# Moving the SBUF tiles of an attention and feed-forward kernel to multiples of 128 bytes

## The chip, the core and the metric

The kernel runs on one core of one Trainium2 chip. The metric is the device time of one execution in microseconds (us): the median of several runs. TensorE (PE) multiplies matrices and writes to PSUM; VectorE (DVE) and ScalarE (ACT) do the element-wise work; SyncE (SP) issues nearly all DMAs; GpSimd (POOL) does a little at the start. SBUF is the on-chip memory that all of them read: 128 partitions, and an address in bytes along each. Every tile has one address, the same in all partitions.

## The reference

Two attention steps, one after the other, and a feed-forward layer on the result, all in float32:

```python
p_packed = sm_attn(p, k, v)                 # 32 packed queries per head attend to k, v
out = sm_attn(q, p_packed, p_packed)        # 576 queries per head attend to the packed rows
x = out.transpose(0, 2, 1, 3).reshape(8 * 576, 512)
h = x @ w_in                                # 512 -> 2048
g = h * (1 / (1 + exp(-1.702 * h)))
return g @ w_out                            # 2048 -> 512
```

There are 8 batches (`b`), 8 heads of 64 columns, and 4608 tokens in all.

## The kernel before

The order of all work is written out by hand in one long table, `order`, of steps such as `(prod, 1, 4, 1, 2, "D")`; a loop at its end calls them one by one, and each engine executes its own instructions in that order. Tiles come from a pool, `wk`, by a tag with a number of buffers: the buffers of a tag lie at fixed SBUF addresses and are used in turn. In the kernel before, a tag gets its addresses at its first use, right behind the tags used earlier, rounded up to 32 bytes.

The feed-forward layer is done in two phases, `ph` 0 and 1, of half of the 2048 hidden columns each, and each phase in four parts `u` of 256 hidden columns. For every phase, batch and half of a batch's 576 tokens (`half`), and every `u`:

- `h_mm` (line 699) makes h in PSUM: 2 times 6 matmuls. The moving operand, which streams through TensorE, is 288 columns of a tile `a` (the attention weights of the second step, split in an upper and a lower part); the stationary operand, which is loaded into TensorE ahead of the matmul, is 128 columns of a tile `m` (packed values times `w_in`, split likewise).
- ScalarE writes the gated result to a tile `X` (line 719); VectorE forms four sums in `X` (line 769); ScalarE and VectorE split the seven blocks of `X` into an upper and a lower part in a tile `gs` (lines 111 and 789).
- `prod` (line 860) multiplies seven blocks of `gs` with seven combinations of the blocks of `w_out`, four in a tile `Wa` and three in a tile `Wb`, by three matmuls each, since both are split: 21 matmuls, into four PSUM banks A to D. The stationary operand is 128 columns of `gs`, the moving one 256 columns of `Wa` or `Wb`. There is one `Wa` and one `Wb` tile for each `u` (tags `Wa0` to `Wa3`, `Wb0` to `Wb3`), and `prod(..., u, "B")` is always six matmuls on the `Wb` tile of that `u`. Tokens 257 to 288 of each half are gathered from several batches as `over` and go the same way.

Batches 1 to 7 give 14 sets of tokens in each phase (two halves each) and the `over` tokens two more (one for every four batches): 16, so 128 passes through `prod` (2 phases, 16 sets, 4 parts), so 2688 matmuls of line 860: 1536 on `Wa`, 1152 on `Wb`. Batch 0 takes a simpler way, `prod0` (line 816): 192 matmuls of 512 moving columns from `Wa`. `h_mm` makes 1536 matmuls.

Around them stand the smaller steps: `m_mm` (line 547, moving operand `w_in`), the scores, softmaxes and transposes of attention (tiles `x`), and DMAs. `k`, `q`, `v` and the partial results of phase 0 are loaded into the two buffers of tag `kqv`; weights come in as `raw`; partial results leave from `r`; four batches send their transposed attention weights through DRAM in pieces of 128 bytes a partition (`aside`).

These are the places, in bytes past a multiple of 256, of the tiles that matter, in the built program of before:

| tile | before |
|---|---|
| `gs` (3 buffers), `X` (3), `r` (2), `PT` (8), `aT` | 128 |
| `Wa0` to `Wa3`, `Wb0`, `Wb1` | 192 |
| `Wb2` | 64 |
| `Wb3` | 128 |
| `m` (3), `a` (3), `x` (6), `kqv` (2), `over` (4) | 192 |
| `raw` (2) | 64 |
| `w_in` (2), `ident`, `minus` | 128 |

All blocks inside these tiles that a matmul of line 860 reads begin at multiples of 512 bytes from the tile's start; the second half of an `a` tile begins 1152 bytes into it, that is 128 past a multiple of 256. The `gs` tile of the very last pass through `prod` is an exception: it takes a buffer of tag `m`.

Of the kernel before, what the change touches and what calls it, by code (L numbers as in the profile page):

```python
# [8 lines left out]
F32 = mybir.dt.float32  # L9
# [12 lines left out]
def kernel(  # L22
# [33 lines left out]
    P = 128  # L56
    D = P // 2
    DM, DF = w_in.shape
    NP = DM // P
    B = q.shape[0]  # L60
    S = q.shape[2] // NP
    NPK = pk.shape[2] // NP - S
    NH = S // 2
    G = S // NPK
    FC = 512
    HC = FC // 2
    CF = FC // P
    KC = (S + P - 1) // P
# [4 lines left out]
    ABUFS, XBUFS, GBUFS, RBUFS = 3, 3, 3, 2  # L73
# [3 lines left out]
    wk = ctx.enter_context(tc.tile_pool(name="wk", bufs=1))  # L77
    ps_acc = ctx.enter_context(tc.tile_pool(name="ps_acc", bufs=1, space=PSUM))
    ps_h = ctx.enter_context(tc.tile_pool(name="ps_h", bufs=2, space=PSUM))
    dram = ctx.enter_context(tc.tile_pool(name="dram", bufs=1, space=bass.MemoryType.DRAM))  # L80

    ident = cst.tile([P, P], F32, name="ident")
    make_identity(nc, ident)
# [84 lines left out]
    raw = {}  # L168
# [1604 lines left out]
```

## Time and profile before

| | us |
|---|---|
| median of 3 runs | 672.59 |
| lowest and highest run | 672.45, 673.4 |
| span of the profiled execution | 672.0 |
| TensorE matmul busy in that span | 658.8 (98%) |
| VectorE busy | 555.0 (83%) |
| ScalarE busy | 409.3 (61%) |

The span is the time from the first to the last instruction of one profiled execution; the runs lie 0.4 to 1.4 us above it. In the rows below, start times count from the start of the span. The busy time of a matmul contains its way through the array, in which the next one already runs. So the pace of TensorE is not read from the length of a matmul (the profile gives about 0.28 us for one of 256 columns) but from start to start.

### The profile page before, as it was taken

To read this page: it belongs to the slowest core of one execution; us is meant where nothing else is said; L and a number is where in the kernel's file an instruction comes from. 1 tells how busy PE (TensorE), PEld (TensorE's weight loads), DVE (VectorE), ACT (ScalarE), POOL (GpSimd) and SP (SyncE) were. 2 spreads that over 40 slices of the span, in tenths; PEclk is the share of its full clock that TensorE was granted. 3 is DMA by queue.
4 is the path that set the end of the run, shared out by engine and by line. 5 is a ranking of instruction groups with operands and counts; after the bars stand their busy time and mean duration, and the time that the engine had idled before them with its cause. 6 is when DMAs were issued, how large, how long until landed. Compare 5 with 4: busy or idle time off the path is not lost.

```text
span 672.0 us, 15271 instructions
## 1 busy us (share of the span) xinstructions
PE 658.8 (98%) x6227; PEld 598.2 (89%) x6227; DVE 555.0 (83%) x1132; ACT 409.3 (61%) x738; POOL 5.4 (1%) x15
## 2 busy tenths in 40 slices
PE   8999899999999999999999999999999999999996
PEld 6777698988989899898999799999999999999996
DVE  3969988879799796987999846878898878886897
ACT  5878777858677695886978554444443544434441
POOL 2100000000000000000000000000000000000000
PEclk9999999999999999999999999999999999999999
DMA  9885646745465476463785315141252222233221
GB/s 342 306 283 182 228 95 222 200 166 217 110 243 144 163 232 188 156 182 137 259 292 187 128 36 155 54 173 50 82 180 88 87 88 87 62 112 87 87 88 63
DMA packets 59174, 104.92 MB, mean 156 GB/s; under 512 B 31392, under 2 KB 36128, under 8 KB 58208
## 3 DMA queue, kind: packets, MB, share of 16 engines
q1 hardware_dynamic: 58960, 103.81, 47.3%
q8 instruction: 49, 0.80, 0.5%
q14 instruction: 21, 0.17, 0.1%
q10 hardware_dynamic: 144, 0.13, 0.1%
HBM read 70.51 MB, written 33.42 MB: 155 GB/s over the span
## 4 chain that ended last, share of the span: by engine, by line
PE 79%; DMA 7%; DVE 7%; ACT 4%; SPq 2%; issue 1%; DVEq 0%; ACTq 0%
PE h L699 25%; PE accC L860 11%; PE accA L860 11%; PE accB L860 10%; PE accD L860 6%; PE psm_None L547 4%; DMA raw_in_None<-w_in 2%; PE accA_over L860 2%; PE accB_over L860 2%; DMA home_m<-w_in 1%; PE accC_over L860 1%; PE ps L591 1%; DMA aT<-aside 1%; PE pspv_None L496 1%; DMA home<-w_in 1%; PE accD L816 1%
## 5 line engine op out<-in xcount | busy, mean ns | idle before, releaser
L699 PE MATMUL h<-a,m 128*128 128x288 f32 x1536 | 223.8, 296 | 2.5 <-ACT x L111 1.3
L699 PEld LDWEIGHTS h<-a,m 128*128 128x128 f32 x1536 | 208.2, 188 | 8.2 <-ACT x L111 2.9
L111 ACT CAST gs<-X 128x896 fp32r<-128x896 f32 (+2 forms) x117 | 104.6, 902 | 75.8 <-DVE X L769 17.8
L789 DVE TENSOR_TENSOR gs<-X,gs 128x896 fp32r<-128x896 f32 x112 | 120.8, 1086 | 22.8 <-ACT gs L111 22.3
L719 ACT ACTIVATE X<-h 128x512 f32<-128x512 f32 (+1 forms) x129 | 76.1, 597 | 83.4 <-PE h L699 77.7
L769 DVE TENSOR_TENSOR X<-X 128x256 f32<-128x256 f32 (+1 forms) x336 | 104.6, 330 | 21.6 <-ACT X L719 17.2
L860 PE MATMUL accC<-Wa,gs 128*128 128x256 f32 x672 | 98.1, 281 | 0.0
L860 PE MATMUL accB<-Wb,gs 128*128 128x256 f32 x672 | 97.7, 281 | 0.0
L860 PEld LDWEIGHTS accC<-Wa,gs 128*128 128x128 f32 x672 | 87.3, 188 | 5.2 <-issue 4.3
L860 PEld LDWEIGHTS accB<-Wb,gs 128*128 128x128 f32 x672 | 87.3, 188 | 1.9 <-issue 0.9
L860 PE MATMUL accA<-Wa,gs 128*128 128x256 f32 x336 | 59.0, 284 | 0.0
L860 PE MATMUL accD<-Wa,gs 128*128 128x256 f32 x336 | 58.5, 282 | 0.0
L860 PE MATMUL accA<-Wb,gs 128*128 128x256 f32 x336 | 57.8, 280 | 0.0
L860 PEld LDWEIGHTS accA<-Wa,gs 128*128 128x128 f32 x336 | 47.7, 188 | 5.4 <-issue 5.1
L860 PEld LDWEIGHTS accD<-Wa,gs 128*128 128x128 f32 x336 | 48.0, 188 | 4.6 <-issue 2.2
L111 ACT CAST m<-psm_None 128x1024 fp32r<-128x1024 f32 x31 | 30.8, 1016 | 29.4 <-PE psm_None L547 29.0
L860 PEld LDWEIGHTS accA<-Wb,gs 128*128 128x128 f32 x336 | 47.5, 188 | 0.0
L571 DVE TENSOR_TENSOR m<-psm_None,m 128x1024 fp32r<-128x1024 f32 x31 | 37.3, 1217 | 6.7 <-ACT m L111 6.5
L725 ACT ACTIVATE over<-h 128x64 f32<-128x64 f32 x128 | 35.3, 289 | 0.0
L547 PE MATMUL psm_None<-w_in,PT 64*32 64x512 f32 x496 | 32.6, 596 | 0.8 <-DVE x L601 0.8
L665 DVE TENSOR_TENSOR a<-xt,a 128x576 fp32r<-128x576 f32 x31 | 23.1, 745 | 2.5 <-ACT a L111 2.1
L719 ACT ACT_TABLE_LOAD x17 | 21.8, 1283 | 4.3 <-PE h L699 3.0
(203 smaller groups left out, 794.4 us busy)
## 6 DMA issues: line engine op xcount, KB each, us to landing
part<-r SPq DMA_DIRECT2D x14, 896.0 KB, 5.4
p<-part SPq DMA_DIRECT2D x14, 896.0 KB, 5.5
q<-q SPq DMA_DIRECT2D x16, 576.0 KB, 5.4
o<-r SPq DMA_DIRECT2D x16, 512.0 KB, 3.5
raw_out_None<-w_out SPq DMA_DIRECT2D x16, 511.8 KB, 5.6
v<-v SPq DMA_DIRECT2D x7, 1024.0 KB, 5.6
raw_in_None<-w_in SPq DMA_DIRECT2D x12, 511.8 KB, 4.8
k<-pk SPq DMA_DIRECT2D x8, 640.0 KB, 4.0
```

Of the source, the lines that this page charges most:

```text
L111: nc.scalar.copy(dst, src)
L496: nc.tensor.matmul(bank[32 * j : 32 * j + 32, e, e * D : (e + 1) * D], turned()[:, c, e, 32 * j : 32 * j + 32], vt[:, c, e0 : e0 + D], sta ...
L547: nc.tensor.matmul(banks[eo][32 * j : 32 * j + 32], PT[rows(eo), j, :], w_in_sb[c % 2][rows(eo), j, at], start=True, stop=True,)
L571: nc.vector.tensor_tensor(m[:, 1, :, at], st["bank", "m", b, c, part], m[:, 0, :, at].bitcast(F32), op=ALU.subtract,)
L591: nc.tensor.matmul(bank[32 * j : 32 * j + 32, eo, :NH], st["PT", b][rows(eo), j, :], kq["q0", half][rows(eo), j, :] if b == 0 else kq["q", ...
L665: engine.tensor_tensor(even_odd(a[:, 1], eo), even_odd(st["t", 2, b, half], eo), even_odd(a[:, 0], eo).bitcast(F32), op=ALU.subtract,)
L699: nc.tensor.matmul(h, m[:, part, eo, at], a[:, ap, eo * NH : (eo + 1) * NH], start=(n == 0), stop=(n == len(terms) - 1), skip_group_check= ...
L719: nc.scalar.activation(X[:, :4].rearrange("p (f t) n -> p f (t n)", f=2)[:, chunks(f)], st["h", *k][:, chunks(f), :NM], AF.Gelu_apprx_sigm ...
L725: nc.scalar.activation(over_part(ph, b, half, u), st["h", ph, b, half, u][:, :, NM:NH], AF.Gelu_apprx_sigmoid, scale=2.0,)
L769: engine.tensor_tensor(to, a, b_, op=ALU.subtract)
L789: engine.tensor_tensor(lo, X, hi.bitcast(F32), op=ALU.subtract)
L860: nc.tensor.matmul(acc[:, n * HC : (n + 1) * HC], gs[:, gp, g], Wa[:, wp, w] if w < 4 else Wb[:, wp, w - 4], start=(u == 0 and n == 0 and ...
```

## The change

Right after the pools are opened, a table `places` takes all buffers of all tags of the pool once, in a chosen order, before the first instruction: the tags of a few bytes first, then a pad of 16 words (64 bytes), then the large ones. That fixes the addresses; nothing is written to or read from these first tiles. Every later use of a tag gets its buffers in the same turn as before.

```diff
     dram = ctx.enter_context(tc.tile_pool(name="dram", bufs=1, space=bass.MemoryType.DRAM))
+
+    places = (
+        ("mx1", 2, 2), ("nb1", 2, 2), ("sm1", 2, 2), ("again", 1, 2), ("rs1", 1, 4), ("rsa", 1, 2),
+        ("mx2", G, 2), ("sm2", G, 2), ("rs2", G, 2), ("pad0", 16, 1),
+        ("kqv", KC * DM, 2), ("x", S, 6), ("Wb2", 6 * HC, 1),
+        ("gs", 14 * P, GBUFS), ("aT", KC * 2 * P, 1), ("X", 8 * P, XBUFS),
+        ("r", 7 * HC, 2), ("pn", 2 * D, 1), ("PT", P, 8), ("Wb3", 6 * HC, 1), ("raw", 2 * FC, RBUFS),
+        ("Wb0", 6 * HC, 1), ("m", 4 * FC, 3),
+    )
+    for tag, words, bufs in places:
+        for i in range(bufs if words else 0):
+            wk.tile([P, words], F32, tag=tag, name=f"place_{tag}_{i}", bufs=bufs)
```

The tags that are not in the table (`Wa0`, `a`, `Wb1`, `over0`, `Wa1` and so on) follow behind `m` in the order of their first use, as before. In the built program every instruction, its engine, its place in the order, its shape and its waits are the same; addresses alone differ. Every tile of the table above now lies at a multiple of 256 bytes, apart from `w_in`, `ident` and `minus`, which stay at 128 past one. The small tiles (maxima, sums and their reciprocals) move by a multiple of 128 bytes. No tile changes its size or its number of buffers.

## Rows read from the trace of the kernel before

**Rows 1.** Page, the chain that ended last, share of the span by engine.

```profile
PE 79%; DMA 7%; DVE 7%; ACT 4%; SPq 2%; issue 1%; DVEq 0%; ACTq 0%
```

**Rows 2.** Stretches: busy us (and instructions) of each engine, PE clock, DMA, GB/s.

```profile
0.00:48.00 48.00, 44.92 (x442) 33.30 (x443) 30.77 (x70) 33.17 (x79) 5.41 (x15) 1.00 0.88 308
...
82.00:368.00 286.00, 284.39 (x3037) 261.10 (x3037) 247.61 (x506) 213.56 (x369) 0.00 (x0) 1.00 0.60 190
...
420.00:645.00 225.00, 225.00 (x1920) 215.25 (x1920) 187.46 (x383) 101.14 (x176) 0.00 (x0) 1.00 0.29 93
645.00:672.00 27.00, 21.34 (x180) 21.14 (x179) 22.34 (x50) 7.11 (x13) 0.00 (x0) 0.94 0.26 93
```

**Rows 3.** Groups by line and shape, VectorE: count, busy us, mean ns, idle before.

```profile
L769 DVE TENSOR_TENSOR X<-X 128x128 f32<-128x128 f32 x224 | 61.0, 285 | 3.1
L769 DVE TENSOR_TENSOR X_over<-over,X_over 128x128 f32<-128x128 f32 x32 | 8.7, 284 | 0.2
```

**Rows 4.** DMA issues: how many, KB each, median us from issue to landing.

```profile
part<-r SPq DMA_DIRECT2D x14, 896.0 KB, 5.4
p<-part SPq DMA_DIRECT2D x14, 896.0 KB, 5.5
aside<-xb SPq DMA_DIRECT2D x48, 72.0 KB, 2.1
```

**Rows 5.** Timeline of PE, 359 to 367.5 us: start, length, matmuls in a row.

```profile
359.02 0.87 PE L860 MATMUL accB_over<-Wb,gs_over 128*128 128x256 f32 x6
359.73 0.87 PE L860 MATMUL accC_over<-Wa,gs_over 128*128 128x256 f32 x6
...
361.85 0.87 PE L860 MATMUL accB_over<-Wb,gs_over 128*128 128x256 f32 x6
362.56 0.52 PE L860 MATMUL accD_over<-Wa,gs_over 128*128 128x256 f32 x3
...
364.67 0.85 PE L860 MATMUL accB_over<-Wb,gs_over 128*128 128x256 f32 x6
365.36 0.52 PE L860 MATMUL accA_over<-Wa,gs_over 128*128 128x256 f32 x3
...
366.77 0.89 PE L860 MATMUL accB_over<-Wb,gs_over 128*128 128x256 f32 x6
367.50 0.28 PE L860 MATMUL accD_over<-Wa,gs_over 128*128 128x256 f32 x1
```

**Rows 6.** Timeline of PE: first and last undisturbed bank B blocks of each class.

```profile
83.02 0.87 PE L860 MATMUL accB<-Wb,gs 128*128 128x256 f32 x6
...
658.45 0.87 PE L860 MATMUL accB_over<-Wb,gs_over 128*128 128x256 f32 x6
...
92.49 0.87 PE L860 MATMUL accB<-Wb,gs 128*128 128x256 f32 x6
...
659.86 0.87 PE L860 MATMUL accB_over<-Wb,gs_over 128*128 128x256 f32 x6
...
142.00 0.88 PE L860 MATMUL accB<-Wb,gs 128*128 128x256 f32 x6
...
653.47 0.88 PE L860 MATMUL accB<-Wb,gs 128*128 128x256 f32 x6
```

**Rows 7.** Timeline of PE: bank B block of the last pass through prod.

```profile
664.09 0.86 PE L860 MATMUL accB_over<-Wb,gs_over 128*128 128x256 f32 x6
664.78 0.39 PE L860 MATMUL accC_over<-Wa,gs_over 128*128 128x256 f32 x2
```

**Rows 8.** The chain that ended last, in order of time: start, us, what.

```profile
375.61 1.40 PE accB L816 x6
...
591.33 4.75 PE h L699 x36
```

**Rows 9.** Groups by line and shape, TensorE.

```profile
L699 PE MATMUL h<-a,m 128*128 128x288 f32 x1536 | 223.8, 296 | 2.5 <-ACT x L111 1.3 <-ACT over L725 1.0
L547 PE MATMUL psm_None<-w_in,PT 64*32 64x512 f32 x496 | 32.6, 596 | 0.8 <-DVE x L601 0.8
```

## The prediction

> **What bounds the kernel now.** I read the chain of work that ended last first: TensorE has 79% of the span, and DMA, VectorE and ScalarE share most of the rest [rows 1]. The table by stretches says where. Up to 48 us the DMA engines are 88% busy and move 308 GB/s; that is the start, which waits for data. [...]
>
> The change alters no instruction, no order and no wait. It can act only through what an access costs at one address or another. So the question to the trace is: do like instructions on tiles at different places differ already?
>
> **VectorE, ScalarE and DMA: nothing found.** Line 769 forms sums of 128x128 blocks from `X` (at 128 past a multiple of 256) in 285 ns and from `over` (at 192) and `X` in 284 ns [rows 3]. DMAs of 896 KB land 5.4 us after issue out of `r` (at 128) and 5.5 us into `kqv` (at 192) [rows 4]. I take zero for both, and that zero is covered: after 82 us VectorE's and ScalarE's slack and DMAs issued ahead hide a per cent on either. Before 48 us DMA is the bound; a tenth of a microsecond in 5.5 us is 2%, and half of the loads of that stretch go to tiles that change, so the end of that zero is about 0.5 us either way (48 x 0.02 / 2).
>
> **TensorE: the pace of line 860.** The moving operands of line 860 lie at three kinds of places before, while the stationary ones (`gs`) always lie at 128: `Wa` of all parts and `Wb` of parts 0 and 1 at 192, `Wb` of part 2 at 64, `Wb` of part 3 at 128. A bank B block is six matmuls on one `Wb` tile; within 8 us one of each part stands in the timeline, and its pace is the start of the next block minus its own, since no wait lies between. Part 0: 359.02 to 359.73, 0.71 us. Part 1: 361.85 to 362.56, 0.71. Part 2: 364.67 to 365.36, 0.69. Part 3: 366.77 to 367.50, 0.73 [rows 5]. The lengths beside them say the same (0.87, 0.87, 0.85, 0.89), and so do the two blocks of part 3 at the ends of the kernel (0.88) [rows 6].
>
> This holds everywhere. Of the bank B blocks that another product follows at once there are 43 on parts 0 and 1 (the first at 83.02, the last at 658.45), mean 705 ns, or 117.5 a matmul; 23 on part 2 (92.49 to 659.86), mean 699, or 116.4; and 20 on part 3 (142.00 to 653.47), mean 716, or 119.3 [rows 6]. The slowest of the 43 takes 710 ns, the fastest of the 20 also 710: the classes hardly touch. [...]
>
> What sets the classes apart? Part 3 is the one in which moving and stationary operand lie at the same place (128 and 128), the others are 64 or 192 apart. The very last pass is a second sign: the moving tile is that of part 3, but `gs` sits in a buffer of tag `m`, at 192, and its block takes 664.09 to 664.78, 0.69 us [rows 7]. It is one block. I take it that the next weights are loaded while the matmul streams, and that the two reads disturb each other most when both start at the same place.
>
> After the change `Wa`, `Wb` and `gs` are all at 0: the same place, as in part 3. So I price every matmul of line 860 at part 3's pace:
>
> - 1536 on `Wa` and 576 on `Wb` of parts 0 and 1 (the `Wa` block at 359.73 has the length of the bank B blocks of parts 0 and 1, 0.87 us [rows 5]): 2112 x (119.3 - 117.5) = 3.8 us.
> - 288 on `Wb` of part 2: 288 x (119.3 - 116.4) = 0.8 us.
> - 288 on `Wb` of part 3: nothing.
> - 192 of `prod0`, 512 columns, 1.40 us for six [rows 8], moving at 192 against `gs` at 128: between 0 and the same loss twice over (twice the columns), 0 to 0.7 us. The loss seems to belong to the loading of one set of weights, so I take it once: 192 x 1.8 ns = 0.35 us.
> - 1536 of `h_mm` [rows 9], 288 columns: 4.75 us for 36, 132 ns each [rows 8]. Here `m` and `a` lie at 192 both (the second half of `a` at 64), and after the change at 0 both (128): the distances stay. I take 0; ends below.
> - `m_mm`: `PT` and `w_in` go from the same place to 128 apart. No row shows that pair; the 496 matmul records of it are 32.6 us busy [rows 9], so a per cent and a half, as in line 860, is 0.5 us either way. I take 0.
>
> The lengths of TensorE's idle stretches give something back: 1.6 us from 82 to 368 us [rows 2] are waits for other engines, which a slower TensorE meets less often. Between 0 and 1.6 us; I take 0.3, since the extra time of that stretch is about half of the total and spread evenly. The sum is 3.8 + 0.8 + 0.35 - 0.3 = 4.7 us on the span of 672.0. The runs lie just above the span (672.45 to 673.4, median 672.59), so I add it there: 677.3 us.
>
> **The rivals.**
>
> Other side, faster: what matters is not sameness but a special pair, and 0 against 0, which no matmul of line 860 has before, is a good one. Part 2's pace is the good one that the trace has. At 116.4 ns everywhere the time falls by 2112 x 1.1 + 288 x 2.9 = 3.2 us, to 669.4 (0.8 of it on the matmuls of part 3). It decides the matter if the block that stood at 366.77 us has under 0.70 us afterwards. At the 0.69 us of the part 2 block in [rows 5], 115 a matmul, it would be 2112 x 2.5 + 288 x 1.4 + 288 x 4.3 = 6.9 us, 665.7. Against it: the one place where both start alike (part 3) is the slowest of all.
>
> No change: the loss of part 3 is not of the place modulo 256, but of where in SBUF `Wb3` lies as a whole (at 122 KB, nearer to `gs` and `X` than the other weights), or of something in part 3's turn. Then nothing that the change does moves it: 672.6, within 1 us. For it: `h_mm` has its operands at like places and no clear loss. The line through 117.5 ns at 256 columns and 233 at 512 gives 132 at 288, just what is measured. That is the strongest sign against my forecast. [...] The trace's 0.69 against 0.73 us for the same work [rows 5] does not agree that nothing in the addresses matters.
>
> Slower than forecast: it is the moving operand alone that is slow at a multiple of 128, whatever the weights do. Then `h_mm`, whose moving operand leaves 192 and 64 for 0 and 128, loses too: 1536 x 1.8 x 288/256 = 3.1 us more, 680.4. Against it stands the last block [rows 7].
>
> [...]
>
> That the change doesn't do what it says is out: in the built program the addresses are where it puts them, and nothing else differs.
>
> **How the numbers follow.** Forecast, line 860 slows to part 3's pace: 0.46, 675 to 678.5 us. Also `h_mm`: 0.10, 679 to 681. No change: 0.21, 671.7 to 673.7. Line 860 faster: 0.19, 665.7 to 671. DMAs: 0.04, 671 to 672.6. A measurement of this kernel tells apart about 0.2%, 1.3 us. Faster by over that: the faster case and half of the DMAs', 0.21; within: no change and the other half, 0.23; slower: 0.56. The range from 669.2 to 681.0 leaves out the lower half of the faster case (0.10) and the ends of the slower ones; the likeliest case's own range is 675 to 678.5.
>
> **What would show it.** In the timeline of after, bank B blocks of all four parts should take 0.71 to 0.73 us from start to start, part 2 no longer less; 36 matmuls of `h_mm` still 4.75 us; VectorE's and ScalarE's groups unchanged to a per cent; TensorE's stretch from 82 us on longer by 4 to 5 us and the first 48 us as before. Blocks at 0.70 us and less, or `h_mm` under 131 ns a matmul, would prove the forecast wrong.

## The result, and the profile after

The changed kernel takes 676.94 us (median of 4 runs, 675.67 to 678.45) against 672.52 us before (4 runs): a ratio of 1.0066, interval 1.0051 to 1.008. It is slower by 4.4 us, as forecast (677.3 us).

The chain of work that ended last, of the changed kernel, in shares of the span by engine; it answers [rows 1]. TensorE has even more of it:

```profile
PE 86%; DVE 5%; ACT 3%; DMA 3%; issue 1%; DVEq 0%; SPq 0%; ACTq 0%
```

The stretches of the changed kernel, with the columns of [rows 2]; the last one runs to the end of the longer span:

```profile
0.00:48.00 48.00, 44.16 (x435) 33.09 (x436) 29.59 (x67) 32.46 (x78) 5.41 (x15) 0.96 0.86 305
82.00:368.00 286.00, 284.66 (x3022) 261.37 (x3021) 246.37 (x503) 211.99 (x367) 0.00 (x0) 1.00 0.58 190
420.00:645.00 225.00, 225.00 (x1905) 215.26 (x1904) 185.89 (x376) 99.94 (x171) 0.00 (x0) 1.00 0.29 95
645.00:676.70 31.70, 26.09 (x216) 25.89 (x214) 25.77 (x60) 9.87 (x18) 0.00 (x0) 0.95 0.22 80
```

TensorE is as full as before and gets fewer matmuls done: 3022 for 3037 from 82 to 368 us, 1905 for 1920 from 420 to 645 us. So each takes longer. Which ones, the timeline of TensorE shows (start, length, matmuls in a row; line 872 is line 860 of before, all lines are 12 later). These are the four bank B blocks that stand in [rows 5], parts 0 to 3 in turn, each with the block behind it:

```profile
361.69 0.88 PE L872 MATMUL accB_over<-Wb,gs_over 128*128 128x256 f32 x6
362.42 0.88 PE L872 MATMUL accC_over<-Wa,gs_over 128*128 128x256 f32 x6
...
364.57 0.88 PE L872 MATMUL accB_over<-Wb,gs_over 128*128 128x256 f32 x6
365.30 0.52 PE L872 MATMUL accD_over<-Wa,gs_over 128*128 128x256 f32 x3
...
367.45 0.88 PE L872 MATMUL accB_over<-Wb,gs_over 128*128 128x256 f32 x6
368.18 0.52 PE L872 MATMUL accA_over<-Wa,gs_over 128*128 128x256 f32 x3
...
369.62 0.88 PE L872 MATMUL accB_over<-Wb,gs_over 128*128 128x256 f32 x6
370.33 0.52 PE L872 MATMUL accD_over<-Wa,gs_over 128*128 128x256 f32 x3
...
668.77 0.88 PE L872 MATMUL accB_over<-Wb,gs_over 128*128 128x256 f32 x6
669.49 1.60 PE L872 MATMUL accC_over<-Wa,gs_over 128*128 128x256 f32 x12
```

From start to start they take 0.73, 0.73, 0.73 and 0.71 us (starts are rounded to 0.01), where parts 0 to 2 took 0.71, 0.71 and 0.69. The three classes have become one: the 87 bank B blocks that another product follows at once have a mean of 718.5 ns, 119.8 a matmul. The last two lines answer [rows 7]: the block of the last pass, 0.69 us before, takes 0.72.

VectorE's sums and the DMAs, in the form of [rows 3] and [rows 4], are the same to 1 ns and to 0.1 us. First the groups of VectorE by line and shape, then the DMA issues, both of the changed kernel:

```profile
L781 DVE TENSOR_TENSOR X<-X 128x128 f32<-128x128 f32 x224 | 61.0, 285 | 3.1
L781 DVE TENSOR_TENSOR X_over<-over,X_over 128x128 f32<-128x128 f32 x32 | 8.7, 283 | 0.2
```

```profile
part<-r SPq DMA_DIRECT2D x14, 896.0 KB, 5.5
p<-part SPq DMA_DIRECT2D x14, 896.0 KB, 5.4
aside<-xb SPq DMA_DIRECT2D x48, 72.0 KB, 2.0
```

Its groups of TensorE as in [rows 9], and behind them the chain in order of time, which answers [rows 8]: `h_mm` and `m_mm` are as busy as before, and 36 matmuls of `h_mm` take the same 4.75 us, but six of `prod0` a little less than their 1.40 us:

```profile
L711 PE MATMUL h<-a,m 128*128 128x288 f32 x1536 | 223.7, 296 | 2.2 <-ACT x L123 1.1 <-ACT over L737 1.0
L559 PE MATMUL psm_None<-w_in,PT 64*32 64x512 f32 x496 | 32.6, 596 | 0.8 <-DVE x L613 0.8
```

```profile
377.06 1.38 PE accD L828 x6
...
379.82 1.36 PE accA L828 x6
...
595.36 4.75 PE h L711 x36
```

### The profile page after: what moved, and what is told of

It reads as the page before. It is cut to its first block, busy times and chain, and to the rows that moved or that the text cites. A ratio compares the mean times of both kernels' runs of the same rounds, so it can differ in the third digit from the quotient of the medians.

```text
span 676.7 us, 15271 instructions
## 1 busy us (share of the span) xinstructions
PE 663.1 (98%) x6227; PEld 603.4 (89%) x6227; DVE 555.8 (82%) x1132; ACT 409.4 (61%) x738; POOL 5.4 (1%) x15
## 4 chain that ended last, share of the span: by engine, by line
PE 86%; DVE 5%; ACT 3%; DMA 3%; issue 1%; DVEq 0%; SPq 0%; ACTq 0%
PE h L711 28%; PE accC L872 12%; PE accA L872 12%; PE accB L872 12%; PE accD L872 6%; PE psm_None L559 4%; DMA raw_in_None<-w_in 2%; PE accA_over L872 2%; PE accB_over L872 2%; PE accC_over L872 1%; PE ps L603 1%; PE accD L828 1%; PE accD_over L872 1%; PE pspv_None L508 1%; PE accC L828 1%
## 5 line engine op out<-in xcount | busy, mean ns | idle before, releaser
L872 PE MATMUL accB<-Wb,gs 128*128 128x256 f32 x672 | 99.1, 283 | 0.0
```

The lines of the kernel that those rows point to most:

```text
L872: nc.tensor.matmul(acc[:, n * HC : (n + 1) * HC], gs[:, gp, g], Wa[:, wp, w] if w < 4 else Wb[:, wp, w - 4], start=(u == 0 and n == 0 and ...
```

## The experiments

The theory on trial: what sets the pace of line 860 is the **distance**, the place of the moving tile (`Wa`, `Wb`) minus that of the stationary one (`gs`), modulo 256. Against it stood that multiples of 128 bytes as such are slow (for the moving operand, or for any), and that the order or region of the tiles is. All kernels but the last are the changed kernel with a few small tags moved inside `places`: a tag of two buffers of 2 words takes 64 bytes, so `mx1` in front of `gs` shifts it by 64, and a tag of 192 bytes behind it puts the next tile back to a multiple of 256. From e2 on the diffs show only the line on trial; the tags that it takes leave the first two lines of the table.

In one table, the paces being the mean time from start to start (ns) of the matmuls that stand between two others of their own line, without a wait behind them (some 2400 of line 860, 1300 of `h_mm`, 156 of `prod0`), each from one profiled execution. The runs lie on several chips, on which the kernel before took 672.5 to 673.3 us, so across rows the ratios compare and not the medians:

| kernel | `gs` / `m` / `a` | distance for line 860 | median us | ratio, interval | line 860 | `h_mm` | `prod0` |
|---|---|---|---|---|---|---|---|
| before | 128 / 192 / 192 | 64; 192 (`Wb2`); 0 (`Wb3`) | 672.5 | 1 | 117.7 | 132.2 | 231.1 |
| changed | 0 / 0 / 0 | 0 | 676.94 | 1.0066 (1.0051 to 1.008) | 119.6 | 132.1 | 228.7 |
| e1_all192 | 192 / 192 / 192 | 0 | 676.57 | 1.0061 (1.0046 to 1.0076) | 119.6 | 132.1 | 228.5 |
| e4_gs192 | 192 / 0 / 0 | 64 | 671.77 | 0.9992 (0.9981 to 1.0002) | 117.3 | 132.0 | 231.3 |
| e3_gs128 | 128 / 0 / 0 | 128 | 675.72 | 1.0043 (1.0028 to 1.0058) | 118.6 | 131.9 | 232.8 |
| e2_gs64 | 64 / 0 / 0 | 192 | 668.7 | 0.9947 (0.993 to 0.9963) | 115.6 | 132.2 | 233.3 |
| e7_gs32 | 32 / 0 / 0 | 224 | 674.14 | 1.0017 (1.0008 to 1.0027) | 118.4 | 132.3 | 233.1 |
| e8_gs96 | 96 / 0 / 0 | 160 | 674.03 | 1.001 (0.9999 to 1.0021) | 117.9 | 132.3 | 234.1 |
| e5_gs64_m64 | 64 / 64 / 0 | 192 | 667.65 | 0.9918 (0.9903 to 0.9933) | 114.9 | 133.0 | 233.4 |
| e6_gs64_m192 | 64 / 192 / 0 | 192 | 665.25 | 0.9885 (0.987 to 0.9899) | 113.9 | 132.8 | 233.2 |
| e10_gs64_m128 | 64 / 128 / 0 | 192 | 669.16 | 0.9939 (0.9923 to 0.9956) | 115.1 | 133.1 | 233.3 |
| e11_gs64_m224 | 64 / 224 / 0 | 192 | 668.2 | 0.992 (0.9901 to 0.9939) | 114.3 | 132.3 | 233.2 |
| e9_gs64_a64 | 64 / 0 / 64 | 192 | 671.5 | 0.9978 (0.9967 to 0.9988) | 116.7 | 132.6 | 233.4 |
| e12_before_gs192 | 192 / 192 / 192 | 0; 128 (`Wb2`); 192 (`Wb3`) | 674.71 | 1.0022 (1.0011 to 1.0033) | 118.8 | 132.0 | 228.5 |

### Alignment or distance: no tile at a multiple of 256, and gs alone away from it

```diff
-        ("mx1", 2, 2), ("nb1", 2, 2), ("sm1", 2, 2), ("again", 1, 2), ("rs1", 1, 4), ("rsa", 1, 2),
-        ("mx2", G, 2), ("sm2", G, 2), ("rs2", G, 2), ("pad0", 16, 1),
+        ("mx1", 2, 2), ("nb1", 2, 2), ("sm1", 2, 2), ("again", 1, 2), ("rs1", 1, 4), ("rsa", 1, 2), ("mx2", G, 2), ("sm2", G, 2), ("rs2", G, 2),
```

> The changed kernel without its 64 bytes of padding: every large tile lies at 192 past a multiple of 256, so none is at a multiple of 128, and all distances between them are those of the changed kernel. If the distance between moving and stationary operand sets the pace: line 860 stays at 119.7 ns a matmul, 676 to 677 us. If the moving operand's own place does (slow at multiples of 128): line 860 returns to 117.5 ns, 671 to 672 us. If neither: 672.5 or 677, with line 860's pace unexplained.

Without the padding every large tile lies 64 bytes before a multiple of 256, and the whole loss stays: 676.57 us. A multiple of 128 or 256 bytes is not what costs. Nor do DMAs that begin at one help: 676.57 without them, 676.94 with them.

```diff
-        ("mx1", 2, 2), ("nb1", 2, 2), ("sm1", 2, 2), ("again", 1, 2), ("rs1", 1, 4), ("rsa", 1, 2),
-        ("mx2", G, 2), ("sm2", G, 2), ("rs2", G, 2), ("pad0", 16, 1),
+        ("nb1", 2, 2), ("sm1", 2, 2), ("again", 1, 2), ("rs1", 1, 4), ("rsa", 1, 2), ("sm2", G, 2), ("rs2", G, 2), ("pad0", 16, 1),
...
-        ("gs", 14 * P, GBUFS), ("aT", KC * 2 * P, 1), ("X", 8 * P, XBUFS),
+        ("mx2", G, 2), ("gs", 14 * P, GBUFS), ("mx1", 2, 2),
...
```

> As before, but gs at 192 past a multiple of 256: weights begin 64 past gs, as Wa, Wb0 and Wb1 did in the kernel before. By distance: 117.6 ns, about 672 us. By the moving operand's place alone: 119.7 ns, 677 us.

Only `gs` leaves its multiple of 256, so that the distance is 64 again, as for most matmuls before. The time is back at that of before, 671.77 us, with every other large tile still at a multiple of 256. So the change's loss is that of this one distance. It is not the place of `gs` by itself either: at 192 it is slow in e1 and not here, and `Wa` and `Wb` at 0 are slow in the changed kernel and not here. The timelines of TensorE show the same block (part 2 of the four above) first with everything at 192, then with `gs` at 192 alone: 0.72 us and 0.71.

```profile
365.84 0.88 PE L872 MATMUL accB_over<-Wb,gs_over 128*128 128x256 f32 x6
366.56 0.52 PE L872 MATMUL accA_over<-Wa,gs_over 128*128 128x256 f32 x3
```

```profile
363.38 0.87 PE L872 MATMUL accB_over<-Wb,gs_over 128*128 128x256 f32 x6
364.09 0.51 PE L872 MATMUL accA_over<-Wa,gs_over 128*128 128x256 f32 x3
```

### The other distances, in steps of 64 and of 32 bytes

```diff
+        ("mx1", 2, 2), ("gs", 14 * P, GBUFS), ("mx2", G, 2),
```

> The changed kernel with the gs tiles alone moved to 64 past a multiple of 256 (the tags of small tiles are spread as padding ahead of and behind them); Wa and Wb stay at 0, so they begin 192 past gs, modulo 256, as Wb2 did in the kernel before. By distance: line 860 at about 116.4 ns for all parts, 8.5 us less than in the changed kernel, about 668.5 us, faster than both. By the moving operand's place alone: 119.7 ns, 677 us.

```diff
+        ("rs1", 1, 4), ("gs", 14 * P, GBUFS), ("again", 1, 2), ("rsa", 1, 2),
```

> As before, but gs at 128 past a multiple of 256: weights begin 128 from gs. No matmul of line 860 has had this distance. By distance modulo 128 it is the same as 0: 119.7 ns, 677 us; by distance modulo 256 it is a pair of its own, between 116 and 120 ns, 667 to 677 us. By the moving operand's place alone: 119.7 ns, 677 us.

A distance of 192, which only `Wb2` had before, is the best: 668.7 us, 8 us below the changed kernel by a shift of one tag. 128 is nearly as bad as 0 (118.6 ns for 119.6). The last pass of e2 is a control inside the same execution, since its `gs` sits in a buffer of `m`, at distance 0. In the timeline of e2 the bank B block of part 2 takes 0.70 us, that of the last pass 0.72:

```profile
361.17 0.87 PE L872 MATMUL accB_over<-Wb,gs_over 128*128 128x256 f32 x6
361.87 0.52 PE L872 MATMUL accA_over<-Wa,gs_over 128*128 128x256 f32 x3
...
658.71 0.88 PE L872 MATMUL accB_over<-Wb,gs_over 128*128 128x256 f32 x6
659.43 1.59 PE L872 MATMUL accC_over<-Wa,gs_over 128*128 128x256 f32 x12
```

```diff
+        ("pad1", 8, 1), ("gs", 14 * P, GBUFS), ("pad2", 8, 1), ("mx2", G, 2),
```

> The changed kernel with gs at 32 past a multiple of 256, so Wa and Wb begin 224 past it. If the distance counts in steps of 64 bytes: line 860 at 119.6 ns (as 0) or 115.6 (as 192), 676.5 or 668.7 us. If it counts finely: between the two, about 117.6 ns, 672.5 us.

```diff
+        ("pad1", 8, 1), ("mx1", 2, 2), ("gs", 14 * P, GBUFS), ("pad2", 8, 1), ("rs1", 1, 4),
```

> As before, but gs at 96, so Wa and Wb begin 160 past it. In steps of 64 bytes: 115.6 ns (as 192) or 118.6 (as 128), 668.7 or 675.7 us. Finely: about 117 ns, 672 us.

Both lie at 674 us, where a fine count was expected to give 672 to 672.5. 224, between 192 (115.6 ns) and 0 (119.6), gives 118.4; 160, between 128 (118.6) and 192, gives 117.9. Steps of 32 bytes count, but neither pace is the mean of its neighbours (117.6 and 117.1).

### The tiles of h_mm, with gs at 64

```diff
+        ("nb1", 2, 2), ("m", 4 * FC, 3), ("sm2", G, 2),
```

> The changed kernel with gs at 64 past a multiple of 256 (as in the run that took 668.7 us) and the m tiles at 64 too; a stays at 0, with its second half at 128. The two distances of h_mm, moving a minus stationary m, become 192 and 64 in place of 0 and 128. If h_mm follows the law of line 860 (119.6 ns at 0, 117.3 at 64, 118.6 at 128, 115.6 at 192): h_mm falls from 132.2 to about 129.5 ns, 4 us less, about 664.7 us. If the law holds only for matmuls of 256 columns: h_mm stays at 132 ns, 668.7 us.

```diff
+        ("sm2", G, 2), ("m", 4 * FC, 3), ("nb1", 2, 2),
```

> As before, but m at 192: the distances of h_mm become 64 and 192, the other way round. By the law of line 860 the mean is the same as with m at 64: 129.5 ns, about 664.7 us. If h_mm does not follow it: 132 ns, 668.7 us. A difference between the two runs would say that the distance to the matmul that follows, not only the set of distances, counts.

```diff
+        ("rs1", 1, 4), ("m", 4 * FC, 3), ("again", 1, 2), ("rsa", 1, 2),
```

> gs at 64 and m at 128, a at 0: the distances of h_mm are 128 and 0, the halves changed over against the changed kernel. If the phase left by h_mm selects the pace of the products behind it, line 860 is anywhere from 113.3 ns (all rows at the good pace) to 117.5 (none), 662.5 to 673.5 us, and rows behind h_mm differ from rows behind other matmuls. If line 860 depends on its own distance alone: 115.6 ns as with m at 0, 668.7 us.

```diff
+        ("pad1", 8, 1), ("sm2", G, 2), ("m", 4 * FC, 3), ("pad2", 8, 1),
```

> gs at 64 and m at 224, a at 0: the distances of h_mm are 32 and 160. The same question as with m at 128: 662.5 to 673.5 us if the phase left by h_mm selects the products' pace, 668.7 us if line 860 depends on its own distance alone. Beside it a search: a pace of h_mm under 132 ns would beat the best run so far, 665.3 us.

```diff
+        ("m", 4 * FC, 3), ("Wa0", 8 * HC, 1), ("nb1", 2, 2), ("a", 2 * S, ABUFS), ("sm2", G, 2),
```

> As the run with gs at 64 and m at 192, but reached the other way: m stays at 0 and the a tiles move to 64, so the distances of h_mm, moving a minus stationary m, are again 64 and 192. In the run with m at 192 the rows of line 860 ran at 113.9 ns against 115.6 with m at 0, though gs, Wa and Wb had the same distance. If distances alone count and a row of products keeps the phase that the h_mm ahead of it leaves: line 860 at 113.9 ns, h_mm at 132.8, 665.3 us. If the place of m counts by itself, through what ScalarE and VectorE write there: line 860 at 115.6 ns, 668.7 us.

`m` at 192 gives the fastest kernel of the study, 665.25 us (665.0 to 665.79), by the ratios 1.15% below before and 1.8% below the changed kernel, with the same instructions in the same order. That is near the 664.7 us expected of a faster `h_mm`, but it does not come by `h_mm`: its own pace never leaves 131.9 to 133.1 ns, and it is not better there (132.8). It is line 860 again, whose tiles and distance are those of e2: 113.9 for 115.6 ns. Of e11 the profiled execution, from which its 114.3 ns is, took 665.56 us; its other three, at a mean clock of 0.995, took 668.1 to 668.5. And moving `a` to 64 (`Wa0` stands in the table only to stay in front of it) makes line 860 slower, 116.7, and the time 671.5 us, neither of the two that were expected. So distance is not the whole of it.

The timelines show that there are two paces. First e9: two rows of line 872 (matmuls of that line with none of another between them) at the same distance, the first behind `prod0`, the second behind `h_mm`, each with its first and its last block. Then the second row again, in e6:

```profile
412.36 0.51 PE L872 MATMUL accD<-Wa,gs 128*128 128x256 f32 x3
...
416.10 0.50 PE L872 MATMUL accA<-Wb,gs 128*128 128x256 f32 x3
416.44 1.75 PE L711 MATMUL h<-a,m 128*128 128x288 f32 x12
...
421.92 0.87 PE L872 MATMUL accC<-Wa,gs 128*128 128x256 f32 x6
...
427.58 0.52 PE L872 MATMUL accA<-Wb,gs 128*128 128x256 f32 x3
427.93 0.87 PE L872 MATMUL accB<-Wb,gs 128*128 128x256 f32 x6
```

```profile
419.85 0.85 PE L872 MATMUL accC<-Wa,gs 128*128 128x256 f32 x6
...
425.63 0.84 PE L872 MATMUL accB<-Wb,gs 128*128 128x256 f32 x6
```

In e9 36 matmuls from 412.36 to 416.44, 113.3 ns each; 51 from 421.92 to 427.93, 117.8. In e6 the same 51, from 419.85 to 425.63, take 113.3. At distances of 0, 64 and 192 a row soon takes a steady pace and as a rule keeps it until a wait disturbs it (with `gs` at 32, 96 and 128, in e7, e8 and e3, the times of a row go on changing, between some 115 and 122 ns). From the 16th matmul of a row on (20 matmuls behind `prod0`, all of one row; some 755 behind `h_mm`, up to some 645 us):

| mean ns | before | changed | e4 | e2 | e5 | e6 | e10 | e11 | e9 |
|---|---|---|---|---|---|---|---|---|---|
| distance | mixed | 0 | 64 | 192 | 192 | 192 | 192 | 192 | 192 |
| behind `prod0` | 113.4 | 120.0 | 113.3 | 113.3 | 113.4 | 113.3 | 117.8 | 113.4 | 113.4 |
| behind `h_mm` | 118.1 | 120.0 | 117.8 | 115.1 | 114.2 | 113.5 | 114.4 | 113.6 | 117.1 |

At distance 0 all rows end at 120.0 ns, whatever came before. At 64 and at 192 there are two paces, about 113.3 and 117.8, and a mean between them is a mixture: in e6 97% of the matmuls behind `h_mm` (from the 16th on) take 114 ns or less, in e2 61%, in e9 14%, in e4 none.

So the distance between the operands of a row says which paces there are. Which one the row gets changes with the places of `m` and `a`, and the line ahead of the row does not settle it, since rows behind `h_mm` take both in e2. The trace of e2 shows what goes with it there: the times of `h_mm` itself go up and down between some 125 and 140 ns, and the point in this rhythm at which it ends differs from row to row. All 14 rows of 16 matmuls and more ahead of which its last two times from start to start are 135 or 136 and then 125 or 126 ns run at 117.8; all but two of the others behind `h_mm` run at 113.3. That is seen, not tested: no run changed the handover alone, e9 also had another distance between `a` and `gs` there, and how the places of `m` and `a` act on it is open.

### The change's loss added to the kernel before

```diff
+    places = (
+        ("kqv", KC * DM, 2), ("x", S, 6), ("mx1", 2, 2), ("nb1", 2, 2), ("Wb2", 6 * HC, 1),
+        ("sm1", 2, 2), ("again", 1, 2), ("gs", 14 * P, GBUFS),
+    )
```

> The kernel before with the gs tiles alone moved up by 64 bytes, to 192 past a multiple of 256 (the tag of two 4-byte tiles is placed ahead of gs and not behind aT; aT moves by 64 too, all else stays). No tile is aligned by it; the distances of Wa, Wb0 and Wb1 from gs become 0, that of Wb2 128, that of Wb3 192. By distance, with the paces of the runs on the changed kernel (119.6 ns at 0, 118.6 at 128, 115.6 at 192): 2112 x 2.0 + 288 x 2.1 - 288 x 3.8 = 3.7 us slower than before, about 676.3 us, the loss of the change without its alignment; bank B blocks of parts 0 and 1 at 716 to 720 ns, of part 3 at 680 to 707. If the loss is of the alignment of all tiles: 672.6 us as before.

On the kernel before, `gs` (and `aT`, behind it) move by 64 bytes and nothing else of size does. It costs 1.9 us (674.71 against 672.79 on that chip), about half of the loss and half of the 3.7 us expected. The paces give some 2.4 us: line 860 gains 118.8 - 117.7 = 1.1 ns, 2.9 us on 2688 matmuls, and `prod0` gives back 0.5. What it lacks to the full loss is the steady pace of the rows. `Wb3` is now at distance 192, and a row that passes through such a block leaves its 120.0 ns: in the timeline of e12 the block of part 3 takes 0.69 us, and of the first 2340 start-to-start times within rows 1069 are 120 ns, against 1574 in the changed kernel.

```profile
366.79 0.88 PE L868 MATMUL accB_over<-Wb,gs_over 128*128 128x256 f32 x6
367.50 0.51 PE L868 MATMUL accA_over<-Wa,gs_over 128*128 128x256 f32 x3
368.91 0.86 PE L868 MATMUL accB_over<-Wb,gs_over 128*128 128x256 f32 x6
369.60 0.51 PE L868 MATMUL accD_over<-Wa,gs_over 128*128 128x256 f32 x3
```

## Why the prediction was right, step by step

- **What bounds the kernel**: right. The forecast adds what line 860 loses to the span whole, and [rows 2], where TensorE is full from 82 to 368 and from 420 to 645 us, carry that. It stays as full (284.66 of 286.00 us and all of 225.00), and what line 860 loses is paid. From 82 us on the execution is 3.6 us longer (the first matmul of line 860 starts 1.1 us later, the span ends 4.7 us later), a little below the 4 to 5 us that were given as a sign: line 860's 4.3 us less the 0.5 and 0.3 us that `prod0` and `h_mm` give back are 3.5.
- **Line 860 at part 3's pace, 4.6 us**: right. Its 2550 matmuls that another of the line follows take 4.3 us more, 304.5 to 308.8, summed from start to start; the pace is 119.6 where 119.3 was taken. That sameness is the cause is shown by e1 (same everywhere, no multiple of 256: the loss stays) and e4 (distance alone undone: the loss goes).
- **Why sameness costs**: the prediction took it that the next weights' load and the stream disturb each other. The length of the loads fits that, but weakly: a load of line 860 has a mean of 188 ns before and in e6 and e3, 190 to 191 in the changed kernel. That is not a proof, and e3 is slow (118.6) with loads of 188 ns. The mechanism stays argued.
- **`prod0`, 0.35 us**: wrong sign. With 512 columns 0 is the fastest and 192 slower than it: 228.7 ns at distance 0, 231.1 to 231.3 at 64, 232.8 at 128, 233.3 at 192. It gave 192 x 2.5 = 0.5 us back. A loss "of the loading of one set of weights" would have shown here too, so that reason falls for 512 columns.
- **`h_mm`, `m_mm`, VectorE, ScalarE, DMA at nothing**: right. `h_mm` changed by 0.3 us in sum (132.21 to 132.14 ns back to back), `m_mm` by nothing, and the sums and transfers are the same.
- **Waits, 0.3 us back**: right. From 82 to 368 us TensorE is idle for 1.3 us where it was 1.6; behind that its idle time changes by less than 0.1 us.
- **The first 48 us as before**: not in the profiled execution, which is 1.4 us behind at 20 us. Its clock was granted at 0.83 from 10 to 20 us, that of the execution of before at 1.00. The stretch of before, then of the changed kernel:

```profile
10.00:20.00 10.00, 9.57 (x168) 6.69 (x169) 6.76 (x22) 7.07 (x22) 2.61 (x4) 1.00 1.03 401
```

```profile
10.00:20.00 10.00, 9.69 (x147) 7.36 (x148) 5.57 (x18) 5.88 (x20) 1.67 (x3) 0.83 1.03 411
```

  e1, at the same distances, shows 1.00 there, and e12, with nearly all tiles of before, 0.83 again; so it comes and goes without the change. Two of the changed kernel's four runs have a mean clock of 0.995 (677.72, 678.45), the others 0.999 and 1.000 (676.17, 675.67). So the loss by addresses alone is rather 3.4 to 4.1 us, the former from these other two, the latter from e1, whose four runs lie within 0.4 us. That the measured 676.94 us comes within 0.4 us of the forecast is in part luck.
- **From span to time, 0.6 us**: a profiled execution that was also timed lies 1.8 us above its span (678.45 for 676.7 here), so the one of before, 672.0, stood for some 673.8 us, above the median of its runs. The addition was right only as the offset of that execution from the median.

**The rivals.** Faster, by a good pair 0 and 0: no block is at 0.70 us or less, and 0 is the worst pair. But the other half of that rival, that part 2's pace is to be had everywhere, is true: e2 gives it with distance 192, and 668.7 us is near its 669.4. No change: refuted by the changed kernel itself, whose parts 0 to 2 take part 3's pace although their tiles stay in their regions of SBUF, and by e4. The line through 117.5 ns at 256 columns and 233 at 512, its strongest sign, was none: at 512 columns distance 0 is the fast one (228.7 ns), and no distance took `h_mm` out of 131.9 to 133.1 ns. Nor is the time independent of where the two operands lie: from 665.25 to 676.94 us by place alone. Slower, by the moving operand at a multiple of 128: e1 has none there and is as slow, and `h_mm`, whose moving operand came to 0 and 128, did not move. DMAs, with 0.04 for 671 to 672.6 us: no run shows such a gain, and the 671 us were the author's estimate, the 672.6 us less all of TensorE's 1.6 us of idle time from 82 to 368 us [rows 2]. `aside` lands in 2.0 us for 2.1, and the time is 676.94 us with large tiles at multiples of 256 bytes, 676.57 with none there (e1).

## What to carry to other kernels

When only addresses change, compare like instructions that already lie on different tiles: the pace from start to start of 86 blocks told the cost of the change before it ran. Where TensorE is full with float32 matmuls of 256 columns, the place of the moving tile minus that of the stationary one can be a knob: it was worth up to 1.8% here, turned by ordering a few tiny tiles, and aligning all tiles alike set it to the worst of the six distances that were measured. Try the distances by measurement, and with the neighbouring products in place, for a pace that holds for one product at one width (256 columns) did not hold for another (288, 512).

## What the runs showed of the hardware that was not expected

- **Steady paces.** At distances 0, 64 and 192 rows of matmuls of 256 columns settle at 113.3, about 117.8 or 120.0 ns. The granted clock was 1.00 from 82 to 368 and from 420 to 645 us (before, changed kernel, e6). That these paces are not a continuum shows in the counts: of the first 2340 times within rows, 1574 are 120 ns in the changed kernel, and in e6 1988 are 113 or 114.
- **The same matmuls at the same distance can run at either pace** (the row of 51 in e9 and e6: 117.8 and 113.3). It was so in the kernel before, too. In its timeline the 36 matmuls behind `prod0`, all at distance 64, run at 113.3 ns, in 4.08 us, while its rows behind `h_mm` have a mean of 118.1:

```profile
415.07 0.50 PE L860 MATMUL accD<-Wa,gs 128*128 128x256 f32 x3
...
418.81 0.51 PE L860 MATMUL accA<-Wb,gs 128*128 128x256 f32 x3
419.15 1.75 PE L699 MATMUL h<-a,m 128*128 128x288 f32 x12
```

- **The order of the distances changes with the width**: 0 is the slowest at 256 columns (119.6 ns) and the fastest at 512 (228.5 to 228.7 ns), and at 288 columns no move of `m` or `a` took the pace out of 131.9 to 133.1 ns. Why is open.
